# Kept block weights reread on ScalarE instead of GpSimd, and block weights made in six pieces

## The chip, the cores and the metric

The kernel runs on one NeuronCore of a Trainium2 chip. Times are device microseconds of one execution; of several runs the median is given. TensorE (PE) does the matrix products, VectorE (DVE), ScalarE (ACT) and GpSimd (POOL) the element work; SyncE (SP), ScalarE and GpSimd issue DMA transfers. Each engine works through its own instructions in order, and an instruction that waits holds up those behind it.

## The reference

For 2048 tokens of width 512 the output is a gated sum of a linear attention and a feed-forward network (FFN):

```python
g = sigmoid((x * gate_w).sum(-1))
q, k, v = split(x @ wqkv)               # 32 heads of 16
pq, pk = q @ w_phi, k @ w_phi           # per head
phi = concat(softmax(p), softmax(-p))   # for q and for k
kv, z = phi_k^T v, sum of phi_k
a = (phi_q kv) / (phi_q z + 1e-6) @ wo
b = relu(x @ w1 + b1)**2 @ w2 + b2      # 1792 hidden
out = g * a + (1 - g) * b
```

## The kernel before, in words

**Arithmetic.** Every fp32 matrix is split in a high part `h` (rounded by ScalarE, line 63) and a low part `l = x - h` (VectorE, line 66). A product is three matmuls: hh, hl, lh. `w_phi` is folded into the key weights ahead of time (`fold`), so that x times one 512 x 1024 matrix gives the 512 key features and the 512 values.

**Two sweeps.** The four blocks of 512 tokens pass through half of the hidden units in the first sweep, through the other half in the second. A work item is one block and one chunk of 128 hidden units: 12 matmuls "up" into the PSUM tile `u` (`w1`), `r = relu(u)`, its square and the split `hh`, `hl` on ScalarE and VectorE, and two items later 12 matmuls "down" into `d` (`w2`). Work is hung into this stream with `at(slot, ...)`: a slot is a half step, two to an item. In the first sweep the stream carries the keys and values, their feature map, and the sum `kv`; in the second the queries and the attention. Between the sweeps `kv` is copied, transposed (`kvt`), and the folded query weights are made (`foldq`).

**Seven products in place of eight.** Keys and values are computed by pairs of token chunks, `n` and `m = n + 2`, eight pairs. A pair is a 2 x 2 block product (2 token chunks, 2 halves of the width, 2 halves of the columns), done with seven block products in the Strassen-Winograd way. The left operands are blocks of x and sums of them (`sums`: x rows loaded to `in`, four adds on GpSimd, split into `sh` and `sl`). The right operands are blocks `a, b, c, d` of the weights and sums of them, made once in `joint`: 1 is a, 2 is c, 3 is d, 5 is b-a, 7 is d-b, 6 and 4 are longer sums. Each comes in two halves `j` of 128 rows, each with a high and a low part (512 KB together). The order of the products in a pair is 1, 2, 6, 5, 7, 3, 4 at half steps 0, 1, 1.5, 2.5, 3, 3.5 and 4.5 of the pair, and a pair takes 5. They accumulate in two PSUM tiles, X (1, 6, 5, 3) and Y (2, 7, 4). After each product X or Y is read out: 1, 6, 5 and 3 by ScalarE alone, 2, 7 and 4 by VectorE, which adds an earlier readout.

**Held and kept.** SBUF holds four of the seven weights (`HELD`). The three `KEPT` ones are stored to DRAM (`wkeep`) and reread for each pair into three slots, `sloto_332`, `sloto_333` and `slotez` (tiles that the second sweep uses otherwise). Six halves rotate through three slots, so a slot that served half number s next serves half s + 3. `again` (line 496) is called after each half product, and its DMA is issued by GpSimd, which also does the adds of `sums`, the scaling of the features (line 280) and two subtractions per half in `joint`.

**Who sets the order.** The code's order gives priorities; a scheduler in the recording layer then orders each engine's instructions by what it expects to be ready, so an instruction can stand ahead of one that was written before it. `high_priority` moves instructions forward. DMA completions share eight semaphores for SP and ScalarE together, so an issue can also wait for an earlier transfer with the same semaphore. After `joint` the `u` tile has a single PSUM bank: the next up products wait until `r` (line 370) has read the last.

Of the kernel before, what the change touches and what calls it, by code (L numbers as in the profile page):

```python
# [16 lines left out]
P = 128  # L17
# [12 lines left out]
HELD = 1, 2, 5, 3  # L30
KEPT = 6, 7, 4
# [3 lines left out]
def tile_gated_mix(ctx: ExitStack, tc: tile.TileContext, xT, xn, wqT, wkT, wphi, wv, wo, w1, b1, w2, b2, gw, out):  # L35
# [133 lines left out]
    def joint(loaded, j):  # L169
        wph, *t = loaded  # L170
        two = lambda a: a.rearrange("p (h c) -> p h c", h=2)
        raw = st["raw"]

        def whole(k):
            ps = bank(f"fold{k}")
            for g in range(NK):
                nc.tensor.matmul(ps[:, g * P:(g + 1) * P], t[g][:, k * P:(k + 1) * P], wph[:, g * P:(g + 1) * P],
                                 start=True, stop=True)
            nc.scalar.activation(two(raw[k])[:, :, :256], two(ps), AF.Copy)

        def operand(i, src, slot=None):
            if i in HELD:
                w, k = "ab"[i > 2], 2 * (HELD.index(i) % 2) + j
                hi, lo = (wpool.tile([P, 512], F32R, tag=f"w{w}{hl}{k}", name=f"w{i}{j}", bufs=1) for hl in "hl")
            else:
                hi, lo = both(st["slots"][slot])
            split(src, hi, lo, nc.scalar, nc.vector)
            st["W"][i, j] = hi, lo
            if i in KEPT:
                nc.gpsimd.dma_start(wkeep[KEPT.index(i), j], st["slots"][slot].bitcast(F32))  # L190

        def sub(eng, o, a, b):
            eng.tensor_tensor(o, a, b, ALU.subtract)

        whole(j)
        whole(2 + j)
        a, b = both(raw[j])
        c, d = both(raw[2 + j])
        operand(1, a)
        operand(2, c)  # L200
        sub(nc.vector, a, b, a)
        sub(nc.gpsimd, b, d, b)
        operand(5, a)
        sub(nc.vector, a, d, a)
        operand(3, d)
        sub(nc.gpsimd, c, c, a)
        operand(7, b, 1)
        operand(4, c, 2)
        operand(6, a, j)
# [190 lines left out]
    def do_joint(j):  # L400
        if j == 0:
            joint_start(st["wT"])
        with tc.issue_after(st["up"].ins):
            joint(st["wT"], j)
        if j == 1:
            banks[:] = [ps_a]
            again(KEPT[1], 0, 2)

# [69 lines left out]
    def sums(p):  # L478
        b, c = divmod(p, 2)
        rows = xT[b].rearrange("p k (h c r) -> p k h c r", h=2, c=2)[:, :, :, c, :]  # L480
        a, d = (stage.tile([P, 2, 2, P], F32, tag="in", name="in") for _ in range(2))
# [287 lines left out]
```

## Time and profile before

| | |
|---|---|
| runs | 543.34, 543.04, 542.16 us; median 543.04 |
| profiled execution | 541.55 us, its span 539.8 us |
| TensorE | 514.8 us busy (95%), 3427 matmuls |
| VectorE | 404.1 us (75%) |
| ScalarE | 257.3 us (48%) |
| GpSimd | 142.6 us (26%) |
| rereads of kept weights | 46 of 512 KB, all issued by GpSimd |

In the profile's rows "PE", "DVE", "ACT", "POOL" are the engines, L511 is a line of the kernel, `p<-sloto,sh` is output and inputs with buffer numbers left out. `sloto` stands for two of the slots, `slotez` for the third. "wkeep" is the copy in DRAM. A wait is put down to what came last.

### The profile page before, as it was taken

Reading aid. Unit: us, or ns where it says so; the run is one execution under the profiler, and the core shown is the slowest. Engines: PE = TensorE matmul, PEld = TensorE weight load, DVE = VectorE, ACT = ScalarE, POOL = GpSimd, SP = SyncE. Lnnn points to the kernel's source line nnn. Section 1 sums busy time; section 2 is a strip of 40 time slices with the busy share of each in tenths; the row PEclk is TensorE's granted clock in tenths of the full one; section 3 lists DMA queues with packets and bytes.
Section 4 is the critical chain, followed back from the end, with each engine's and each line's share of the span. In section 5 each row is a group of like instructions: output and inputs, shape, how many; then the busy total and the mean of one; then the engine's idle time right before and its main releaser. Section 6 shows DMA issues by size and latency. Waiting matters only on the chain.

```text
span 539.8 us, 9228 instructions
## 1 busy us (share of the span) xinstructions
PE 514.8 (95%) x3427; PEld 411.8 (76%) x3427; DVE 404.1 (75%) x682; ACT 257.3 (48%) x454; POOL 142.6 (26%) x149
## 2 busy tenths in 40 slices
PE   8978879997999979999899999999999999999997
PEld 4866658886888858878687887878787878888775
DVE  4599498776478636686798779899789887788723
ACT  3985544554345434354555473555444534343540
POOL 2045444155514271422030322121212020111100
PEclk9998979999999989999999999999999999999999
DMA  7968665655266545495438313124311321023112
GB/s 258 301 221 277 210 215 211 197 180 195 80 223 225 178 145 207 137 306 199 139 75 255 102 45 94 46 96 137 84 41 49 100 75 45 15 83 94 31 30 78
DMA packets 47284, 76.64 MB, mean 142 GB/s; under 512 B 6792, under 2 KB 22664, under 8 KB 47240
## 3 DMA queue, kind: packets, MB, share of 16 engines
q1 hardware_dynamic: 39288, 48.39, 28.9%
q0 software_dynamic: 7520, 27.27, 14.7%
q8 instruction: 27, 0.44, 0.3%
q10 hardware_dynamic: 432, 0.39, 0.2%
q14 instruction: 17, 0.14, 0.1%
HBM read 58.20 MB, written 11.54 MB: 129 GB/s over the span
## 4 chain that ended last, share of the span: by engine, by line
PE 60%; DMA 14%; DVE 12%; ACT 5%; issue 4%; POOL 3%; SPq 0%; DVEq 0%; POOLq 0%
PE u L71 6%; PE d L71 6%; PE d L72 6%; PE d L73 6%; PE u L72 6%; PE u L73 6%; DMA in<-in_xT 4%; DMA in<-in_w 3%; DMA slotez<-wkeep 3%; PE q L71 3%; PE att L71 3%; PE att L72 3%; PE att L73 3%; PE q L73 3%; PE q L72 3%
## 5 line engine op out<-in xcount | busy, mean ns | idle before, releaser
L71 PE MATMUL u<-xh,w1h 128*128 128x512 f32 x220 | 88.0, 400 | 5.5 <-ACT r L370 2.8
L299 POOL TENSOR_TENSOR ez<-e,z 128x512 f32<-128x512 f32 x32 | 41.8, 1326 | 183.3 <-ACT e L271 183.3
L71 PE MATMUL d<-w2h,hh 128*128 128x512 f32 x224 | 88.6, 395 | 0.0
L72 PE MATMUL d<-w2l,hh 128*128 128x512 f32 x224 | 88.2, 394 | 0.0
L73 PE MATMUL d<-w2h,hl 128*128 128x512 f32 x224 | 88.1, 393 | 0.0
L72 PE MATMUL u<-xl,w1h 128*128 128x512 f32 x220 | 86.3, 392 | 0.0
L73 PE MATMUL u<-xh,w1l 128*128 128x512 f32 x220 | 85.9, 391 | 0.2 <-DVE w1l L66 0.2
L370 ACT ACTIVATE r<-u,b1c 128x512 f32<-128x512 f32 x56 | 38.3, 684 | 96.4 <-PE u L73 92.9
L66 DVE TENSOR_TENSOR hl<-r,hh 128x512 fp32r<-128x512 f32 x56 | 45.6, 814 | 23.6 <-ACT hh L63 23.6
L71 PEld LDWEIGHTS u<-xh,w1h 128*128 128x128 f32 x220 | 41.5, 189 | 18.6 <-ACT r L370 3.8
L71 PEld LDWEIGHTS d<-w2h,hh 128*128 128x128 f32 x224 | 42.8, 191 | 9.3 <-issue 0.4
L73 PEld LDWEIGHTS d<-w2h,hl 128*128 128x128 f32 x224 | 42.6, 190 | 9.1
L72 PEld LDWEIGHTS d<-w2l,hh 128*128 128x128 f32 x224 | 42.6, 190 | 8.9
L73 PEld LDWEIGHTS u<-xh,w1l 128*128 128x128 f32 x220 | 41.6, 189 | 9.5 <-DVE w1l L66 0.6
L323 ACT ACTIVATE phiT<-tb 32x256 f32<-32x256 f32 x64 | 26.5, 414 | 46.1 <-DVE tb L317 45.5
L72 PEld LDWEIGHTS u<-xl,w1h 128*128 128x128 f32 x220 | 41.6, 189 | 8.0
L274 DVE TENSOR_REDUCE sm<-e 128x64 f32<-128x1024 f32 x27 | 32.8, 1214 | 17.7 <-ACT e L271 17.7
L271 ACT ACTIVATE e<-e 128x1024 f32<-128x1024 f32 x27 | 28.6, 1057 | 21.0 <-DVE e L269 19.1
L63 ACT ACTIVATE hh<-r 128x512 fp32r<-128x512 f32 x56 | 35.2, 628 | 1.2
L371 ACT ACTIVATE r<-r 128x512 f32<-128x512 f32 x56 | 35.1, 626 | 1.1
L280 POOL TENSOR_TENSOR e<-e,r 128x1024 f32<-128x1024 f32 x11 | 22.8, 2071 | 28.5 <-DVE r L276 28.4
L301 DVE TENSOR_REDUCE dz<-ez 128x64 f32<-128x1024 f32 x16 | 19.3, 1204 | 10.9 <-POOL ez L299 10.9
(170 smaller groups left out, 1020.6 us busy)
## 6 DMA issues: line engine op xcount, KB each, us to landing
sloto<-wkeep POOLq DMA_DIRECT2D x30, 512.0 KB, 4.8
in<-in_xT SPq DMA_DIRECT2D x48, 256.0 KB, 4.2
slotez<-wkeep POOLq DMA_DIRECT2D x16, 512.0 KB, 4.5
in<-in_w SPq DMA_DIRECT2D x24, 256.0 KB, 3.3
phiT<-tb SPq DMA_DIRECT2D x192, 32.0 KB, 1.9
row<-in_xn SPq DMA_DIRECT2D x16, 256.0 KB, 3.9
part<-row SPq DMA_DIRECT2D x16, 256.0 KB, 3.8
row<-part SPq DMA_DIRECT2D x16, 256.0 KB, 3.2
```

The source lines that it names most:

```text
L63: i = nc.scalar.activation(hi, src, AF.Copy)
L66: elo.tensor_tensor(lo, src, hi.bitcast(F32), ALU.subtract)
L71: nc.tensor.matmul(o, ah[:, sa], bh[:, sb], start=first, stop=False)
L72: nc.tensor.matmul(o, ah[:, sa], bl[:, sb], start=False, stop=False)
L73: return nc.tensor.matmul(o, al[:, sa], bh[:, sb], start=False, stop=last)
L271: nc.scalar.activation(ef, ef, AF.Exp)
L274: nc.vector.tensor_reduce(sm, e3, AX.X, ALU.add)
L280: eng.tensor_tensor(e3, e3, w.unsqueeze(2).to_broadcast([P, 2 * H, DH]), ALU.mult)
L299: nc.gpsimd.tensor_tensor(ez[:, hs, :], e3[:, hs, :], zbc[half], ALU.mult)
L323: nc.scalar.activation(dst, src, AF.Copy)
L370: nc.scalar.activation(r, ps, AF.Relu, bias=b1c[:, fc:fc + 1])
L371: nc.scalar.activation(r, r, AF.Square)
```

## The change

Three things change. The kept weights are now those of products 1, 6 and 3, which ScalarE reads out; `again` is called once per product, after the readout, rereads two halves, and its DMAs are issued by ScalarE. `joint` is cut in three pieces for each half j, and the six pieces are called at half steps 3, 4, 5, 6, 7 and 8 where two calls stood at 3 and 4. The pairs start at half step 9.5 + 5p where it was 8.5 + 5p; the load of x for `sums` has a call of its own at the half step at which it was, and the adds come 1.5 half steps later.

```diff
-HELD = 1, 2, 5, 3
-KEPT = 6, 7, 4
+HELD = 2, 4, 5, 7
+KEPT = 1, 6, 3
...
+    def joint(j, piece):
+        if piece == 0:
+            whole(j)
+            whole(2 + j)
         a, b = both(raw[j])
         c, d = both(raw[2 + j])
-        operand(1, a)
-        operand(2, c)
-        sub(nc.vector, a, b, a)
-        sub(nc.gpsimd, b, d, b)
-        operand(5, a)
-        sub(nc.vector, a, d, a)
-        operand(3, d)
-        sub(nc.gpsimd, c, c, a)
-        operand(7, b, 1)
-        operand(4, c, 2)
-        operand(6, a, j)
+        if piece == 0:
+            operand(3, j, d, j)
+            operand(1, j, a, j)
+            sub(nc.vector, a, b, a)
+            sub(nc.gpsimd, b, d, b)
+        elif piece == 1:
+            operand(5, j, a)
+            operand(2, j, c)
+            sub(nc.vector, a, d, a)
+        else:
+            operand(7, j, b)
+            sub(nc.gpsimd, c, c, a)
+            operand(4, j, c)
+            operand(6, j, a, 2)
...
-    def again(i, j, slot):
-        t = st["slots"][slot]
-        nc.gpsimd.dma_start(t.bitcast(F32), wkeep[KEPT.index(i), j])
-        st["W"][i, j] = both(t)
+    def again(p, i):
+        for j in range(2):
+            step = 2 * KEPT.index(i) + j
+            nxt, t = step + 3, st["slots"][step % 3]
+            if nxt < 6 or p < NB * NC // 2 - 1:
+                k, jj = KEPT[nxt % 6 // 2], nxt % 2
+                nc.scalar.dma_start(t.bitcast(F32), wkeep[KEPT.index(k), jj])
+                st["W"][k, jj] = both(t)
...
-            if i in KEPT:
-                step = 2 * KEPT.index(i) + j
-                nxt = step + 3
-                if nxt < 6 or p < NB * NC // 2 - 1:
-                    again(KEPT[nxt % 6 // 2], nxt % 2, step % 3)
...
+            if i in KEPT:
+                again(p, i)
...
-        at(s - 1 - (p > 0), sums, p)
+        at(s - 2 - (p > 0), sums_load, p)
+        at(s - 1.5 if p else s - 0.5, sums, p)
...
-    at(3, do_joint, 0)
-    at(4, do_joint, 1)
+    for slot, j, piece in ((3, 0, 0), (4, 1, 0), (5, 0, 1), (6, 1, 1), (7, 1, 2), (8, 0, 2)):
+        at(slot, do_joint, j, piece)
...
-        pair_steps(p, 8.5 + 5 * p)
+        pair_steps(p, 9.5 + 5 * p)
```

In the slots, half 0 of weight 3, then half 0 of weight 1 pass through `sloto_332`, their halves 1 through `sloto_333`; both halves of weight 6, first 1, then 0, through `slotez`. Each is stored to DRAM by GpSimd before the next overwrites it.

GpSimd, in the first sweep at the sums of two later pairs, before:

```order
L280 TENSOR_TENSOR e<-e,r 128x1024
L486 TENSOR_TENSOR in<-in 128x2x128 x2
L487 TENSOR_TENSOR in<-in 128x2x128 x2
L488 TENSOR_TENSOR in<-in 128x2x128 x2
L489 TENSOR_TENSOR in<-in 128x2x128 x2
L498 DMA slotez<-wkeep 128x1024
L498 DMA sloto_332<-wkeep 128x1024
L498 DMA sloto_333<-wkeep 128x1024
```

and at such a place in the changed kernel:

```order
L280 TENSOR_TENSOR e<-e,r 128x1024
L488 TENSOR_TENSOR in<-in 128x2x128
L489 TENSOR_TENSOR in<-in 128x2x128
L280 TENSOR_TENSOR tmp<-tmp,r 128x1024
L490 TENSOR_TENSOR in<-in 128x2x128
L491 TENSOR_TENSOR in<-in 128x2x128
```

The rereads have left GpSimd's queue. They stand on ScalarE, here at products 1 and 6 of pair 1 (line 548 reads a product out):

```order
L548 ACTIVATE tmp<-p_831 128x512
L504 DMA sloto_332<-wkeep 128x1024
L504 DMA sloto_333<-wkeep 128x1024
L271 ACTIVATE e<-e 128x1024
L370 ACTIVATE r<-u,b1c 128x512
L371 ACTIVATE r<-r 128x512
L63 ACTIVATE hh<-r 128x512
L504 DMA slotez<-wkeep 128x1024
L548 ACTIVATE tmp<-p_831 128x512
L504 DMA sloto_332<-wkeep 128x1024
```

The first two are issued after the readout of product 1, the third ahead of that of product 6; it waits for TensorE alone.

ScalarE where the weights are made, in the changed kernel, from the split of the second half of weight 1 on (`sh` are the sums of pair 0; `w_517`, split from `tmp` here, is half 1 of weight 4, `slotez` half 1 of weight 6):

```order
L63 ACTIVATE sloto_333<-tmp 128x512
L63 ACTIVATE w_542<-raw_335 128x512
L63 ACTIVATE sh<-in 128x512 x2
L370 ACTIVATE r<-u,b1c 128x512
L63 ACTIVATE w_477<-tmp 128x512
L371 ACTIVATE r<-r 128x512
L63 ACTIVATE w_512<-tmp 128x512
L63 ACTIVATE hh<-r 128x512
L63 ACTIVATE w_547<-raw_337 128x512
L63 ACTIVATE slotez<-tmp 128x512
L63 ACTIVATE w_517<-tmp 128x512
L370 ACTIVATE r<-u,b1c 128x512
```

Before, 18 splits and folds stood in one run ahead of a single `r`; now two `r` lie within this stretch, the first behind `sh`, the second behind `w_517`. A little further on the first reread of weight 3 and the split of `slotez` from `raw_335` (half 0 of weight 6) stand between the readout of product 1 and the reread of weight 6:

```order
L548 ACTIVATE tmp<-p_595 128x512
L504 DMA sloto_333<-wkeep 128x1024
L63 ACTIVATE slotez<-raw_335 128x512
L504 DMA sloto_332<-wkeep 128x1024
L238 ACTIVATE ge<-lg 128x1 x2
```

All four are new at this place.

60 lines of the change are left out of this document (28 added, 32 removed).

## The prediction, on record before the changed kernel ran

> **What bounds the kernel now.** I read the page's table of engines first.
>
> ```profile
> span 539.8 us, 9228 instructions
> ...
> PE 514.8 (95%) x3427; PEld 411.8 (76%) x3427; DVE 404.1 (75%) x682; ACT 257.3 (48%) x454; POOL 142.6 (26%) x149
> ```
>
> TensorE is busy 95%, so only its 25 us of idle time, and time in which it runs slowly, can be won. The waits of TensorE name the idle time.
>
> ```profile
> PE p L511 <- DMA slotez<-wkeep: 6.1, 3, 3.1
> PE p L511 <- DMA sloto<-wkeep: 4.0, 2, 3.7
> PE u L71 <- ACT r L370: 2.8, 1, 2.8
> PE u L71 <- ACT w1h L63: 2.6, 2, 1.9
> PE foldq L146 <- ACT r L370: 1.6, 1, 1.6
> ...
> PE p L513 <- DVE sl L66: 1.0, 1, 1.0
> PE p L511 <- DVE vext L537: 0.6, 1, 0.6
> PE kvt L597 <- DVE row L586: 0.5, 1, 0.5
> ```
>
> The columns are total, times, longest. Ten microseconds are waits for rereads of kept weights; 6.5 (2.8 + 1.9 + 1.0 + 0.6, and 0.2 below) fall where block weights are made and pair 0 runs; 2.2 (1.63 + 0.53) in the turn to the second sweep. The rest lies in the kernel's first 10 us. TensorE's timeline shows where, and what follows a wait (start, duration, in brackets the idle time before).
>
> ```profile
> 35.01 0.39 PE L72 MATMUL d<-w2l,hh 128*128 128x512 f32 x1
> 38.18 0.51 PE L71 MATMUL u<-xh,w1h 128*128 128x512 f32 x1 [2.78 <-ACT r L370]
> ...
> 45.18 0.50 PE L71 MATMUL u<-xh,w1h 128*128 128x512 f32 x1 [1.90 <-ACT w1h L63]
> ...
> 46.35 0.50 PE L73 MATMUL u<-xh,w1l 128*128 128x512 f32 x1 [0.21 <-DVE w1l L66]
> ...
> 50.34 0.40 PE L71 MATMUL u<-xh,w1h 128*128 128x512 f32 x1
> ...
> 75.05 0.80 PE L511 MATMUL p<-slotez,xh 128*128 128x512 f32 x1 [2.44 <-DMA slotez<-wkeep]
> ...
> 81.06 0.40 PE L513 MATMUL p<-w,xl 128*128 128x512 f32 x1
> ...
> 130.48 0.50 PE L511 MATMUL p<-slotez,xh 128*128 128x512 f32 x1 [3.13 <-DMA slotez<-wkeep]
> 130.81 0.39 PE L512 MATMUL p<-slotez,xh 128*128 128x512 f32 x1
> 131.04 0.39 PE L513 MATMUL p<-slotez,xl 128*128 128x512 f32 x1
> ...
> 193.25 0.57 PE L511 MATMUL p<-sloto,sh 128*128 128x512 f32 x1 [3.66 <-DMA sloto<-wkeep]
> ...
> 197.00 0.40 PE L71 MATMUL d<-w2h,hh 128*128 128x512 f32 x1
> ...
> 235.28 0.50 PE L511 MATMUL p<-slotez,xh 128*128 128x512 f32 x1 [0.56 <-DMA slotez<-wkeep]
> ```
>
> A matmul follows the one before by 0.23 us (130.81 to 131.04). After three of the waits it follows at about 0.4: from 46.35 to 50.34 lie 10 steps (4.0 us instead of 2.3), from 75.05 to 81.06 lie 14 (6.0 instead of 3.2), from 193.25 to 197.00 lie 9 (3.75 instead of 2.0). These slow stretches cost 1.7 + 2.8 + 1.7 = 6.3 us. With 18.8 us of waits between 27 and 300 us (10.1 + 6.5 + 2.2), that is **25.1 us to be won**, and a microsecond of waiting costs on average 1.33.
>
> The rereads are late because of GpSimd, as its timeline shows ("DMA_DIRECT2D" is the issue).
>
> ```profile
> 70.04 1.07 POOL L489 TENSOR_TENSOR in<-in 128x256 f32<-128x256 f32 x1
> 71.05 0.55 POOL L498 DMA_DIRECT2D slotez<-wkeep  x1
> ...
> 126.15 0.57 POOL L498 DMA_DIRECT2D slotez<-wkeep  x1
> ...
> 185.62 0.74 POOL L486 TENSOR_TENSOR in<-in 128x256 f32<-128x256 f32 x1 [11.05 <-DMA in<-in_xT]
> ...
> 189.25 0.55 POOL L498 DMA_DIRECT2D sloto<-wkeep  x1
> ...
> 228.21 0.53 POOL L498 DMA_DIRECT2D slotez<-wkeep  x1 [4.52 <-PE p L513]
> ```
>
> Before 71.05, 126.15 and 189.25 the issue stands behind the adds of a later pair's x, the last of which waited 11 us for x. Those three issues precede the waits that end at 75.05, 130.48 and 193.25. Only the fourth, at 228.21, was issued at once; its transfer took 7.0 us and cost 0.56.
>
> **The change, part by part.** *Rereads, pairs 1 to 7.* Some 45 issues leave GpSimd's queue, and with it the adds. ScalarE issues them; in its order the urgent one of two stands in front of the product's readout (waiting for TensorE alone) or right behind it. What the transfer needs:
>
> ```profile
> DMA to landing us min/median/max: 3.6/4.7/7.7
> ...
> L449 ACTq DMA_DIRECT2D row<-in_w x2: 408/434/459, 0.7 to 1.2; - x2
> ```
>
> The first row is line 498's own, the second the only ScalarE issues that the trace has from the start of a row. From the end of a kept product to the second half that its slot serves next, the new order of TensorE has 27 to 30 matmuls, 6.1 to 6.8 us at 0.227. No 512 KB load on ScalarE's queue is in this trace. Its landing is bounded by the row's 3.6 and 7.7; I take 4.7, the same bytes. Issue (0.43) and landing make 5.1, so most fit, and the waits of pairs 1 to 7 (3.13 + 3.66 + 0.56) go. For 14 such loads I keep 1.5 us, some 0.1 each (bounds 0, and 14 x 1.9 = 27 at 7.7). ScalarE pays 45 x 0.43 = 19 us, hidden in the time in which it waits for TensorE:
>
> ```profile
> ACT r L370 <- PE u L73: 92.9, 28, 8.1
> ```
>
> Without that cover r, and with it the single PSUM bank of the up products, would come 0.4 us later per issue.
>
> The Trainium skill ("DMA: Bandwidth & Descriptors", section "Anatomy of one DMA — SWDGE (gpsimd) path") fits a transfer as 2.0 us and its bytes at 436 GB/s, an estimate of 3.2 us for 512 KB; the row above says 4.7. By the page's figure the 1.5 us would be nothing and the time 2 us lower; I go by the row.
>
> *Weights in six pieces.* The work is the same (14 splits, 4 folds, 8 subtractions), later and spread. What it runs into:
>
> ```profile
> 26.24 0.59 ACT L179 ACTIVATE raw<-fold 128x512 f32<-128x512 f32 x1
> ...
> 37.46 0.67 ACT L370 ACTIVATE r<-u,b1c 128x512 f32<-128x512 f32 x1
> ...
> 41.07 1.67 POOL L193 TENSOR_TENSOR tmp<-tmp 128x512 f32<-128x512 f32 x1 [1.05 <-DVE tmp L193]
> ...
> L488 POOL TENSOR_TENSOR in<-in x8: 729/907/1229, 51.9 to 192.4; 128x256 f32<-128x256 f32 x8
> ...
> in<-in_xT SPq DMA_DIRECT2D x48, 256.0 KB, 4.2
> ...
> wkeep<-slotez POOLq DMA_DIRECT2D x2, 512.0 KB, 4.0
> ```
>
> (a) 18 activations stood from 26.24 to the r at 37.46; 13 do now, at some 0.55 us, with waits for two weight loads: r at about 34.1, done 34.8. TensorE comes there 5 matmuls sooner, at 34.1. The 2.78 becomes 0.7. The 1.9 and 0.2 for w1h go, since its staging buffer now comes free when xl is split, ahead of the weights' splits.
>
> (b) The next r now stands behind both sh splits of pair 0, and these behind GpSimd's four adds. x for them is issued near 33.5 when w2's split frees the buffer, lands 4.2 later, four adds take 4 x 1.1 (upper half of their row, since VectorE is busy too): the second sh is done near 43, r near 43.8. TensorE finishes up at 37.6 and 12 down matmuls at 40.3, a wait of 3.5. With the better adds (4 x 0.75) it is 1.7; I take 2.6 (bounds 0 and 4.5).
>
> (c) The r after it stands behind w4's second split, this behind a GpSimd subtraction (1.67), this behind the adds of pair 1: one more 4 x 1.1 and a third subtraction after 43, so r near 52; TensorE, which has 18 matmuls for cover, waits 1.5 (bounds 0 and 4).
>
> (d) Product 6 of pair 0 needs its second half from DRAM. It is stored by GpSimd right after (c)'s subtraction (4.0 to landing); ScalarE, in order, waits for that store to overwrite the slot with the first half, and only then issues the reread, behind the reread of product 3: 52 + 0.6 + 4 for the store, 0.6 for the split, 4.7 and a little more for the load, near 62. TensorE, which goes on at 53 after (c), is there 21 matmuls later, about 58. I take 3.8 (bounds 0 and 6). This takes the place of the old 0.35 (the rest of "sloto") and 2.44, and the 1.0 for sl and 0.6 for vext go with their later products.
>
> *Pairs half a step later.* This gives (b) to (d) the little cover that they have. At the far end it takes cover away: kv of the last pair now ends 13 matmuls, 3 us, before the transposition that needs it, where it had 20.
>
> ```profile
> 283.94 1.71 DVE L586 COPY row<-kvps 17x256 f32<-17x256 f32 x4
> ```
>
> The copies between them take 1.71 behind whatever VectorE has queued. For that and the folds of q I keep 2.0 of the old 2.2 (bounds 0.5 and 5).
>
> **Sum.** New waits 0.7 + 2.6 + 1.5 + 3.8 + 1.5 + 2.0 = 12.1, with the slow stretches x 1.33 = 16.1. The profiled execution took 541.55 (539.8 and 1.75 around it): 541.55 - 25.1 + 16.1 = 532.6. The median of the runs, 543.04, lies 1.5 above it: **534 us**.
>
> The slow stretches need a word. In the rows, 1.9 and 0.2 brought one, 2.78 and 3.13 none. The Trainium skill ("TensorE: Matmul & The Clock Gate", section "Why this matters for your kernels") has the clock drop only after gaps of more than about 3 us. The trace agrees for 3.66 and not for 1.9 or 3.13. By the page's rule only (d) would bring one, 1.7 us in place of 4, and the time would be 532; I go by the average of the rows.
>
> **The rivals.**
>
> *The new wait stays short* (0.14). GpSimd's adds run faster than my estimate, so that (b) to (d) vanish: 0.7 + 1.5 + 2.0 = 4.2, x 1.33 = 5.6, 541.55 - 25.1 + 5.6 + 1.5 = 523.5. For it: the scheduler put those instructions there because it expects them in time. Against it: VectorE, the third column of times below, was busy 13.19 of 13.5 us there, and its work is the same.
>
> ```profile
> 27.00:40.50 13.50, 10.72 (x56) 8.82 (x55) 13.19 (x18) 11.73 (x22) 6.22 (x6) 1.00 0.63 220
> ```
>
> *All of the making's waits stay* (0.15). (a) to (d) at their upper bounds, 0.7 + 4.5 + 4 + 6, with 1.5 and 2.0: 18.7 x 1.33 = 24.9, time 543, no change. For it: the chain through GpSimd, a store and a load is new and serial. Against it: four bounds at once.
>
> *The reread lands late from ScalarE's queue* (0.14), the slower case. Place: the second halves of products 6 and 1, 14 times. Cover is 6.4 us on average less 0.43, so beyond a landing of 5.9 each further microsecond costs 14 x 1.33 = 18.6 us. It eats my gain of 9 at a mean landing of about 6.5 (1.5 us are in the sum already); at 6.8 the time is 14 x 0.9 x 1.33 - 2 = 15 us above mine, 549. For it: 7.0 at 228.21, when x was loading too, and two loads now start together. Against it: the median of 46 loads.
>
> The skill's page on DMA (section "Issuing engines are not separate DMA queues") has all issuers share the same engines, so the landing should not change with the issuer; no run here shows it yet.
>
> That the change does not do what it says is shut out by the order of GpSimd and ScalarE.
>
> **How the numbers follow.** Forecast 0.57, with its own range 527 to 540 (one of (b) to (d) at a bound either way). From the rivals, 523.5 weighs 0.14, 543 0.15 and 549 0.14. The range of 8 in 10 is 523.5 to 543.5. A measurement of this kernel tells a change from none at about 0.2%, 1.1 us. Faster: 0.57 + 0.14 + a third of 0.15 = 0.76. Same: 0.07. Slower: 0.14 and the rest of 0.15, 0.17.
>
> **What would show it.** Steps that are right: no wait of TensorE for wkeep over 1 us after pair 0; no reread issue on GpSimd; landings of ScalarE's rereads near 4.7; one wait for wkeep in pair 0's product 6 near 4 us; waits of u for r near 2.6 and 1.5 behind sh and w4. Wrong: many waits for wkeep of about a microsecond (third rival), or r waiting for ScalarE's transfers elsewhere in the sweep, which I have costed at nothing.

## The result, and the profile after

The changed kernel takes 546.89 us (median of 20 runs, 541.99 to 549.48), the kernel before 542.06 us beside it (20 runs, 538.28 to 545.38). The ratio is 1.0079, with a 95% interval of 1.0055 to 1.0104: **slower by 0.8%**, a small change, but the interval leaves out 1. 534 us was forecast. The profiled execution took 546.88 us.

The page's table of engines, of the changed kernel:

```profile
span 545.1 us, 9200 instructions
...
PE 516.5 (95%) x3427; PEld 414.3 (76%) x3427; DVE 410.6 (75%) x682; ACT 257.4 (47%) x454; POOL 117.5 (22%) x103
```

GpSimd lost 25 us of work, as intended, and TensorE gained nothing: it is idle 28.6 us (25.0 before) and busy 1.7 us longer for the same number of matmuls. In what follows `r` names two things: the relu of line 370, for which the up products wait, and the reciprocal of line 276, by which GpSimd scales the features. The waits of TensorE (total, times, longest):

```profile
PE u L71 <- ACT r L370: 8.8, 4, 3.7
PE kvps L289 <- POOL e L280: 7.5, 2, 5.4
PE kvt L601 <- DVE row L590: 3.4, 1, 3.4
PE kvps L289 <- issue: 1.2, 1, 1.2
...
PE p L517 <- DMA sloto<-wkeep: 0.9, 2, 0.6
```

The 10.1 us of waits for rereads are 0.9. Two rows are new as waits: 7.5 us in which the kv products (`kvps`, line 289) wait for the scaling of the features by `r` (line 280, GpSimd), and 3.4 us for the transposes at the turn. A third is a gap: 1.2 us ahead of the last two of pair 0's 128 kv matmuls, for which the profile names no releaser ("issue"); the scaling for them had ended at 96.4, and a gap of 0.9 to 1.1 us stays there in e5, e12 and e18 below, which change the order or drop loads. TensorE's timeline has the places, and the slow stretches behind them (start, duration, idle time before):

```profile
37.73 0.50 PE L71 MATMUL u<-xh,w1h 128*128 128x512 f32 x1 [3.32 <-ACT r L370]
...
46.26 0.50 PE L71 MATMUL u<-xh,w1h 128*128 128x512 f32 x1 [1.17 <-ACT r L370]
...
57.10 0.79 PE L71 MATMUL u<-xh,w1h 128*128 128x512 f32 x1 [3.75 <-ACT r L370]
...
62.39 0.63 PE L71 MATMUL u<-xh,w1h 128*128 128x512 f32 x1
...
65.48 0.50 PE L517 MATMUL p<-sloto,sh 128*128 128x512 f32 x1 [0.56 <-DMA sloto<-wkeep]
...
98.35 0.23 PE L289 MATMUL kvps<-e,vext 128*17 128x32 f32 x2 [1.20 <-issue]
...
128.71 1.06 PE L289 MATMUL kvps<-e,vext 128*17 128x32 f32 x64 [5.44 <-POOL e L280]
129.69 0.80 PE L517 MATMUL p<-w,sh 128*128 128x512 f32 x1
...
134.13 0.63 PE L72 MATMUL u<-xl,w1h 128*128 128x512 f32 x1
...
207.26 0.73 PE L289 MATMUL kvps<-e,vext 128*17 128x32 f32 x64 [2.01 <-POOL e L280]
...
291.29 0.41 PE L601 MATMUL kvt<-ident,row 128*128 128x128 f32 x2 [3.42 <-DVE row L590]
```

From 57.10 to 62.39 lie 12 steps (5.3 us instead of 2.7), from 129.69 to 134.13 lie 10 (4.4 instead of 2.3); two more stretches, behind the waits that end at 37.73 and 291.29, cost some 1.5 each. In all the slow stretches cost about 8 us, 6.3 before. Idle time up by 3.6 and slow time up by some 2 make the 5.3 us by which the span grew.

How far TensorE has come by 65 us shows in the busy time between 27 and 65 us; the first figure behind the stretch's length is TensorE's, with its matmuls. The kernel before:

```profile
27.00:65.00 38.00, 31.75 (x136) 24.55 (x135) 31.76 (x63) 25.56 (x50) 19.89 (x21) 0.96 0.71 236
```

and the changed kernel:

```profile
27.00:65.00 38.00, 29.69 (x115) 22.91 (x113) 34.71 (x56) 23.79 (x46) 22.56 (x22) 0.87 0.64 213
```

It is 21 matmuls behind, 4.8 us at 0.227. So nearly the whole loss against the kernel before arises while the weights are made. From there on the rereads' waits go, and waits for kv and for the turn take their place.

How the longest of them comes about can be followed backwards. GpSimd's timeline:

```profile
120.44 0.74 POOL L488 TENSOR_TENSOR in<-in 128x256 f32<-128x256 f32 x1 [1.97 <-DMA in<-in_xT]
...
125.24 0.72 POOL L488 TENSOR_TENSOR in<-in 128x256 f32<-128x256 f32 x1 [0.85 <-DMA in<-in_xT]
126.05 0.72 POOL L489 TENSOR_TENSOR in<-in 128x256 f32<-128x256 f32 x1
126.72 1.93 POOL L280 TENSOR_TENSOR e<-e,r 128x1024 f32<-128x1024 f32 x1
```

Six adds, four for pair 3 and two for pair 4, stand ahead of the scaling of pair 1, and wait for their x. VectorE's timeline shows that `r` for this scaling was done at 122.2, and why it was no sooner:

```profile
106.22 0.69 DVE L236 SCALAR_TENSOR_TENSOR row<-row,gwb 128x512 f32<-128x512 f32 x1 [4.42 <-DMA row<-in_xn]
...
116.90 2.11 DVE L66 TENSOR_TENSOR sl<-in,sh 128x512 fp32r<-128x512 f32 x1
...
121.65 0.54 DVE L276 RECIPROCAL r<-sm 128x64 f32<-128x64 f32 x1
```

VectorE stood 4.4 us at a row of the gate (`in_xn`, line 236), with the pair's readouts and splits queued behind. SyncE issued these rows late, behind loads of x, and the x of pairs 3 and 4 later still, since their staging buffers are free only after VectorE's splits `sl` (for which SyncE waits there):

```profile
99.63 1.74 SPq L81 DMA_DIRECT2D in<-in_xT  x2
101.42 5.86 SPq L231 DMA_DIRECT2D row<-in_xn  x3
113.01 6.43 SPq L482 DMA_DIRECT2D in<-in_xT  x4
```

### The profile page after: what moved, and what is told of

Same layout as the page of the kernel before. It is cut to its first block, busy times and chain, and to the rows that moved or that the text cites. A ratio compares the mean times of both kernels' runs of the same rounds, so it can differ in the third digit from the quotient of the medians.

```text
span 545.1 us, 9200 instructions
## 1 busy us (share of the span) xinstructions
PE 516.5 (95%) x3427; PEld 414.3 (76%) x3427; DVE 410.6 (75%) x682; ACT 257.4 (47%) x454; POOL 117.5 (22%) x103
## 4 chain that ended last, share of the span: by engine, by line
PE 57%; DVE 18%; DMA 12%; ACT 4%; POOL 4%; issue 4%; SPq 1%; ACTq 0%; DVEq 0%; POOLq 0%
PE u L71 6%; PE d L71 6%; PE d L73 6%; PE d L72 6%; PE u L72 6%; PE u L73 5%; DMA in<-in_xT 3%; DMA in<-in_w 3%; DVE sl L66 3%; PE att L73 3%; PE att L71 3%; PE q L72 3%; PE q L73 3%; PE q L71 3%; PE att L72 3%
## 5 line engine op out<-in xcount | busy, mean ns | idle before, releaser
L71 PE MATMUL u<-xh,w1h 128*128 128x512 f32 x220 | 89.4, 406 | 9.0 <-ACT r L370 8.8
L72 PE MATMUL u<-xl,w1h 128*128 128x512 f32 x220 | 87.7, 399 | 0.0
L73 PE MATMUL u<-xh,w1l 128*128 128x512 f32 x220 | 87.4, 398 | 0.0
L66 DVE TENSOR_TENSOR hl<-r,hh 128x512 fp32r<-128x512 f32 x56 | 42.4, 757 | 23.5 <-ACT hh L63 23.5
L280 POOL TENSOR_TENSOR e<-e,r 128x1024 f32<-128x1024 f32 x11 | 24.0, 2179 | 87.7 <-DVE r L276 71.2
L271 ACT ACTIVATE e<-e 128x1024 f32<-128x1024 f32 x27 | 28.6, 1059 | 24.5 <-DVE e L269 22.7
L723 DVE SCALAR_TENSOR_TENSOR row<-d,rest,row 128x512 f32<-128x512 f32 (+1 forms) x33 | 22.5, 726 | 7.8 <-PE d L73 7.8
```

The source lines that it names most:

```text
L66: elo.tensor_tensor(lo, src, hi.bitcast(F32), ALU.subtract)
L71: nc.tensor.matmul(o, ah[:, sa], bh[:, sb], start=first, stop=False)
L72: nc.tensor.matmul(o, ah[:, sa], bl[:, sb], start=False, stop=False)
L73: return nc.tensor.matmul(o, al[:, sa], bh[:, sb], start=False, stop=last)
L271: nc.scalar.activation(ef, ef, AF.Exp)
L280: eng.tensor_tensor(e3, e3, w.unsqueeze(2).to_broadcast([P, 2 * H, DH]), ALU.mult)
```

## The experiments

The theories that the expectations name: **A**, the adds on GpSimd, which run up to two pairs ahead, stand ahead of the scaling for kv. **B**, the loss comes from the pairs' half step or the weight pieces. **C**, ScalarE's DMA issues hold up the exponentials. **D**, VectorE is late in any case, since its list waits for rows of the gate. Every ratio below is to the kernel before on the same chip. The runs are of several chips, on which the kernel before took 541.2 to 544.3 us, so runs are compared by their ratios; a difference of two medians can be off by up to 3 us.

| run | kernel | median us | ratio, 95% interval |
|---|---|---|---|
| | changed kernel | 546.9 | 1.0079 (1.0055 to 1.0104) |
| e1 | changed, sums back behind their loads | 543.0 | 0.9975 (0.9934 to 1.0017) |
| e2 | changed, pairs half a step earlier | 536.7 | 0.9872 (0.9816 to 0.9929) |
| e3 | changed, rereads by GpSimd | 550.1 | 1.0102 (1.0046 to 1.0158) |
| e4 | before, rereads by ScalarE | 534.0 | 0.9830 (0.9770 to 0.9890) |
| e5 | changed, adds in order | 541.9 | 0.9998 (0.9967 to 1.0030) |
| e6 | e4, pairs late | 535.8 | 0.9889 (0.9827 to 0.9952) |
| e7 | e2, pieces bunched | 533.0 | 0.9826 (0.9771 to 0.9882) |
| **e8** | **e4, adds in order** | **524.1** | **0.9668 (0.9620 to 0.9716)** |
| e9 | before, adds in order | 540.3 | 0.9973 (0.9947 to 0.9999) |
| e10 | changed, pairs early, bunched, adds in order | 534.0 | 0.9834 (0.9784 to 0.9884) |
| e11 | changed, pairs early, adds in order | 532.7 | 0.9822 (0.9778 to 0.9866) |
| e12 | changed, bunched, adds in order | 541.0 | 0.9975 (0.9948 to 1.0003) |
| e13 | e8, six pieces | 531.1 | 0.9782 (0.9732 to 0.9833) |
| e14 | e8, pairs late | 536.1 | 0.9852 (0.9805 to 0.9898) |
| e15 | e8, both | 537.2 | 0.9889 (0.9849 to 0.9929) |
| e16 | e14 without rows of the gate | 527.7 | 0.9747 (0.9706 to 0.9789) |
| e17 | e8 without rows of the gate | 524.7 | 0.9694 (0.9655 to 0.9732) |
| e18 | changed, without rows of the gate | 535.0 | 0.9883 (0.9841 to 0.9925) |

### One part undone, one part alone (e1 to e4)

**e1**, against the changed kernel:

```diff
-        at(s - 1.5 if p else s - 0.5, sums, p)
+        at(s - 2 - (p > 0), sums, p)
```

> The changed kernel with the adds and splits of every pair's sums put back right behind their loads, as the kernel before had them; rereads, weight pieces and pairs stay as changed. Theory A (GpSimd works its list in order, and the later adds, which wait for their loads, stand ahead of the scaling by r that the kv products wait for): the kv products' wait for GpSimd, 7.5 us in two places, falls under 2 us, the slow matmuls behind the 5.4 us wait go with it, and the time falls by 7 to 10 us, to 537 to 540. Theory B (the loss comes from the pairs' half step or from the weight pieces): the time stays within 1.5 us of the changed kernel's 546.9. Theory C (ScalarE's six DMA issues a pair hold up the exponentials): the same as B, and the wait of the kv products stays.

543.0 us, 1.0% below the changed kernel's ratio, and a partial answer: the kv products wait 4.0 us (3.2 + 0.8) where they waited 7.5, and 3.5 us of waits for rereads came up (0.9). This edit takes away about half of the wait, and the time lies between the ranges; neither A nor B holds alone.

**e2**, against the changed kernel:

```diff
-        pair_steps(p, 9.5 + 5 * p)
+        pair_steps(p, 8.5 + 5 * p)
```

> The changed kernel with every pair one half step earlier, as before; the sums keep their place relative to the pair. Theory A: the adds stand in the same place relative to the scaling, so the kv products still wait 4 to 8 us; only the 3.4 us wait of the transposes behind the last kv products falls to 0.5, as in the kernel before, and the time is 542 to 545. Theory B (the half step itself is the loss): 538 to 541, kv waits gone. Either way the waits for the weights' making can only grow, since pair 0 starts one half step sooner: 8.8 us of waits for r becomes 9 to 12.

536.7 us, under both ranges (2.1% below the changed kernel by the ratios). The kv products' waits are 2.0 us and the transposes' 0.5; the waits in the making grew as expected, to 5.0 for `r` and 7.1 for weight 6, and yet the kernel is faster. It does not refute A: in this kernel's trace the next adds begin at 123.79, behind the scaling of pair 1 at 121.66.

**e3**, against the changed kernel:

```diff
-                nc.scalar.dma_start(t.bitcast(F32), wkeep[KEPT.index(k), jj])
+                nc.gpsimd.dma_start(t.bitcast(F32), wkeep[KEPT.index(k), jj])
```

> The changed kernel with the rereads issued by GpSimd again, two at the end of each product, in the changed order of the kept weights. If ScalarE as the issuer is what took away the 10.1 us of waits for rereads (my prediction's term), 6 to 10 us of such waits come back, and the time is 553 to 559. If the order of the products and their pairing is enough, the waits for rereads stay under 2 us and the time within 1.5 us of 546.9. Theory C (ScalarE's issues hold up the exponentials) alone says faster: 540 to 544, with the kv wait under 2 us.

550.1 us; its waits of TensorE:

```profile
PE p L517 <- DMA sloto<-wkeep: 11.9, 4, 5.8
PE u L71 <- ACT r L370: 7.5, 3, 3.8
```

The waits for rereads are back at 11.9 us, so ScalarE as issuer is what removed them. But the time rose by 0.2% only, under the range and less than the runs can tell: the kv products now wait for nothing. **A wait for a reread covers the scaling behind which kv would wait: take the first away and the second appears.** C is not decided here: the kv wait goes, as C says too, but the time is no lower, since the rereads' waits are back. It falls with e5 and e8, in which ScalarE issues the rereads and the kv products wait 1.2 and 1.1 us for the scaling.

**e4**, against the kernel before:

```diff
-        nc.gpsimd.dma_start(t.bitcast(F32), wkeep[KEPT.index(i), j])
+        nc.scalar.dma_start(t.bitcast(F32), wkeep[KEPT.index(i), j])
```

> The kernel before with nothing changed but the engine that issues the rereads: ScalarE instead of GpSimd. My prediction's term (10.1 us of waits for rereads, each us worth 1.33 with its slow matmuls) stands alone here: 528 to 531 if the waits go and nothing takes their place. The rival (the time that is won is waited elsewhere, for r and for the weights' making, in the steps that follow): waits for rereads under 2 us, other waits up by 5 us or more, and a time of 537 to 542.

534.0 us, between the two ranges. Of the waits of TensorE:

```profile
PE kvps L289 <- POOL e L280: 6.1, 3, 3.9
...
PE p L511 <- DMA slotez<-wkeep: 1.2, 1, 1.2
```

The rereads' 10.1 us are 1.4, and 6.1 us of waits of the kv products stand where there were none. One word of the diff wins 1.7%; the rest of the change loses 2.5%.

### The order of the adds (e5, e8, e9)

**e5**, against the changed kernel (`scaled` and `phi` record the instruction; the loads of x stay where they were):

```diff
-        add(d1, a1, d1, ALU.add)
-        add(a1, a0, a1, ALU.subtract)
-        add(a0, d1, a0, ALU.subtract)
-        add(d0, d0, a0, ALU.subtract)
+        with tc.issue_after((st["scaled", p - 2] if p > 1 else st["up"]).ins):
+            add(d1, a1, d1, ALU.add)
+            add(a1, a0, a1, ALU.subtract)
+            add(a0, d1, a0, ALU.subtract)
+            add(d0, d0, a0, ALU.subtract)
...
                 v["phi", t] = scaled(e3, r, nc.gpsimd)
+                st["scaled", p] = st["scaled"]
```

> The changed kernel with one order added on GpSimd: the four adds of pair p's sums come behind the scaling of pair p - 2, and so never two pairs ahead of their use. Same operations, same half steps. Theory A (adds for pairs 3 and 4, waiting for their loads, stand ahead of the scaling of pair 1): the kv products' wait for GpSimd, 7.5 us, falls to 1.5 us or less, the slow matmuls behind it go too, and the time is 536 to 540. Theory D (VectorE is late with r in any case, since its list waits 4.4 us for a row of the gate): r itself is late, the kv products still wait 3 us or more, as they did for 4.0 us with the sums put back, and the time is 542 to 546. A new wait for the split sums (sl) of 1 to 3 us would show that the adds now come too late.

541.9 us, ratio 0.9998 against 1.0079. The waits of TensorE:

```profile
PE u L71 <- ACT r L370: 7.9, 3, 3.5
PE p L518 <- DMA sloto<-wkeep: 4.4, 2, 3.5
PE kvt L603 <- DVE row L592: 3.5, 1, 3.5
PE p L518 <- DVE vext L539: 2.1, 1, 2.1
PE kvps L289 <- POOL e L280: 1.2, 1, 1.2
```

The kv products' wait for the scaling fell to 1.2 us as A says. The time fell less than A says: 4.4 us of waits for rereads came up, 3.5 of them for weight 6 in pair 0, and 2.1 us for a readout by VectorE. That last wait would fit D; this run does not show its cause.

**e8** is e4 with the edit of e5, the load of x split off but at its old half step.

> The kernel before with ScalarE issuing the rereads and the adds of pair p put behind the scaling of pair p - 2, nothing else. Theory A: of the 6.1 us that the kv products wait with ScalarE's rereads alone, 4 us or more go, and the time falls from 534.0 to 527 to 531. Theory D: the kv products wait as before and the time stays at 533 to 536.

524.1 us, better than the expectation: 3.3% under the kernel before, 4.1% under the changed one, and the fastest kernel of this study. Its waits of TensorE, and the stretch from 27 to 65 us:

```profile
PE u L71 <- ACT r L370: 2.8, 1, 2.8
PE u L71 <- ACT w1h L63: 2.2, 2, 2.0
...
PE kvps L289 <- POOL e L280: 1.1, 1, 1.1
PE p L515 <- DMA slotez<-wkeep: 1.1, 1, 1.1
```

```profile
27.00:65.00 38.00, 33.06 (x144) 26.25 (x142) 32.24 (x58) 24.90 (x48) 17.18 (x18) 0.96 0.79 258
```

All waits of kv but one are gone, hardly a new one came up (0.6 us for a readout), and one slow stretch is left in the sweep (1.4 us). TensorE has done 144 matmuls by 65 us, 29 more than in the changed kernel.

**e9** is the edit of e5 on the kernel before, with GpSimd still issuing the rereads.

> The kernel before, its rereads still issued by GpSimd, with the adds of pair p put behind the scaling of pair p - 2 and nothing else. It divides the gain of the fastest kernel so far (524.1 us: this order and ScalarE's rereads together) between the two. If the rereads were late only because adds for later pairs, which wait for their loads, stood ahead of their issues, the order alone takes away most of the 10.1 us of waits for rereads and the time is 526 to 531. If GpSimd is too slow an issuer in any case (its scalings, which wait for r, stand ahead of the issues as well), waits for rereads of 5 us or more stay, and the time is 533 to 541.

540.3 us, 0.3% under the kernel before: the waits for rereads are as the first theory has them, 2.7 us, the time is in the range of the second. The kv products wait 2.5, `foldq` 2.5 for `r`, and readouts by ScalarE cost 3.4. So ScalarE's issue alone is worth 1.7%, the order of the adds alone 0.3%, both together 3.3%: with one alone, other waits take up what it wins.

### The half step and the six pieces, with the adds in order (e6, e7, e10 to e15)

**e6** is e4 with `pair_steps(p, 9.5 + 5 * p)`.

> The kernel before with two edits: ScalarE issues the rereads, and every pair comes one half step later. Against ScalarE's rereads alone (534.0 us) it shows the half step by itself, without the six pieces and without the later adds. If the half step is what costs (theory B): 541 to 546, with 3 us of wait for the transposes behind the last kv products and more waits of the kv products than 6.1 us. If it costs only together with the later adds (theory A): 533 to 537, the transposes' 3 us and their slow matmuls aside.

535.8 us, 0.6% above e4 by the ratios, within their intervals. The transposes wait 2.9 us, as expected, but the kv products' wait of 6.1 us is 0.5. Here GpSimd's adds before that scaling run from 101.96 on, where e4 has them from 109.45, and the scaling comes in time. That this hides a part of the half step's price fits e14, where nothing hides it; no run shows it by itself.

**e7** is e2 with the pieces called at two half steps, in the same order:

```diff
-    for slot, j, piece in ((3, 0, 0), (4, 1, 0), (5, 0, 1), (6, 1, 1), (7, 1, 2), (8, 0, 2)):
+    for slot, j, piece in ((3, 0, 0), (3, 0, 1), (4, 1, 0), (4, 1, 1), (4, 1, 2), (4, 0, 2)):
```

> The changed kernel with the pairs at their old half step and the six pieces of the weights' making bunched at half steps 3 and 4 instead of 3 to 8, in the same order of pieces. Against the pairs put back alone (536.7 us) it shows the spreading by itself. If the spreading is a loss (the last piece comes so late that pair 0 waits 7.1 us for the weights of product 6): that wait falls under 2 us, the waits for r stay near 5, and the time is 528 to 532. If the spreading helps, as I predicted (each relu waits less): the waits for r rise by 3 us or more, and the time is 535 to 540.

533.0 us against 536.7, with overlapping intervals: the wait for weight 6 fell from 7.1 to 3.7 us and the waits for `r` stayed (4.9 against 5.0), but kv waits 3.6 in place of 2.0. The run misses both theories, and the times give no clear verdict.

**e10, e11, e12** are the changed kernel with the adds in order (e5), and the pairs, the pieces or both put back.

> The changed kernel with three things put back or in order: pairs at their old half step, six pieces bunched at half steps 3 and 4, adds behind the scaling of pair p - 2. What is left of the change is ScalarE as issuer, the other choice of kept weights, and the order in which the weights are made. Against 524.1 us (the kernel before with ScalarE's rereads and the same order of adds) it shows what the choice of weights is worth. If nothing: 523 to 526. If the new order of making is a loss (weight 6 is made last, and pair 0 needs it third: 3.7 us of wait with the pieces bunched): 527 to 532, with that wait still there.

> The changed kernel with the pairs at their old half step and the adds behind the scaling of pair p - 2; the six pieces stay spread over half steps 3 to 8. Two comparisons: against the same order of adds with the pairs late (541.9 us) it is the half step alone, against the run with the pieces bunched as well it is the spreading alone. If the half step costs by itself (transposes 3 us, and more): 531 to 536. If it gives cover to the making, as I predicted: pair 0 waits 5 us or more for weight 6, and the time is 537 to 542. Spreading: a loss if this is 3 us or more above the bunched one.

> The changed kernel with the pieces bunched at half steps 3 and 4 and the adds behind the scaling of pair p - 2; the pairs stay one half step late. Against 541.9 us (pieces spread) it is the spreading alone with pairs late. If spreading costs (each late piece makes relu or product 6 of pair 0 wait): the waits for r (7.9 us) and for the reread of weight 6 in pair 0 (3.5 us) fall by 5 us or more together, and the time is 531 to 536. If it is harmless: 539 to 543.

In e11 pair 0 waits 5.2 us for weight 6, as was expected of an early pair, and the time is the lower one all the same. With the adds in order the four make a square (medians, us):

| new choice of weights | pairs early | pairs late |
|---|---|---|
| pieces bunched | 534.0 (e10) | 541.0 (e12) |
| pieces spread | 532.7 (e11) | 541.9 (e5) |

The half step costs 7 and 9 us (1.4% and 1.8% by the ratios), the spreading nothing that the runs can tell. And e10 is above e8 (524.1), and above its own ranges: **1.7% by the ratios, 9 us**. What differs is the choice of the kept weights with the order in which they are made; with it go the rereads, two at a time behind the readout, and for the sums x loaded one half step earlier and added half a one later. Its stretch from 27 to 65 us:

```profile
27.00:65.00 38.00, 28.02 (x113) 21.90 (x113) 31.62 (x54) 22.12 (x42) 18.62 (x18) 0.87 0.72 235
```

113 matmuls against 144: 31 of them, 7.0 of the 9 us. TensorE waits 6.6 us in three places for `r` and 3.4 for weight 6, with 3.3 us of slow matmuls after them; weight 6 is made last there, and pair 0 needs it third.

**e13** is e8 with its weights made in six pieces in their old order (1 and 2; 5 and 3; 7, 4 and 6); **e14** is e8 with pairs late; **e15** has both:

```diff
-    at(3, do_joint, 0)
-    at(4, do_joint, 1)
+    for slot, j, piece in ((3, 0, 0), (4, 1, 0), (5, 0, 1), (6, 1, 1), (7, 0, 2), (8, 1, 2)):
+        at(slot, do_joint, j, piece)
```

> The fastest kernel so far (the kernel before, ScalarE's rereads, adds behind the scaling of pair p - 2: 524.1 us) with its weights made in six pieces at half steps 3 to 8, in its own order and with its own choice of kept weights. It shows the spreading by itself. If the changed kernel lost its 7 us before 65 us by the spreading: TensorE has done 115 to 120 matmuls between 27 and 65 us instead of 144, and the time is 530 to 535. If it lost them by the new choice and order of weights (weight 6 last and needed third, its second half through DRAM): 135 to 145 matmuls, 522 to 527.

> The fastest kernel so far (524.1 us) with every pair one half step later, nothing else. The half step alone: it costs the wait for the transposes (2.9 us with 1.3 of slow matmuls after it, as in the earlier run with ScalarE's rereads) and nothing more if kv and the rereads keep their cover: 526 to 530. If the half step brings pairs and the gate's rows together on VectorE (8 to 9 us, as it did with the new choice of weights): 531 to 535.

> The fastest kernel so far (524.1 us) with both: six pieces spread over half steps 3 to 8 and every pair one half step later, the old choice and order of weights. If the two edits add up from the two runs beside this one, spreading and half step do not depend on each other, and what is left to 541.9 us (the changed kernel with the same order of adds) is the price of the new choice and order of weights. If the half step gives cover to the spread making, this is faster than the spreading alone.

| old choice of weights | pairs early | pairs late |
|---|---|---|
| two calls | 524.1 (e8) | 536.1 (e14) |
| pieces spread | 531.1 (e13) | 537.2 (e15) |

Here the spreading alone costs 7 us (1.1% by the ratios, 6 us): 116 matmuls between 27 and 65 us.

```profile
27.00:65.00 38.00, 29.59 (x116) 22.90 (x116) 34.95 (x61) 22.34 (x44) 17.33 (x18) 0.83 0.69 229
```

TensorE waits 4.5 us there for one `r`, at 53.72. In ScalarE's list splits stand ahead of it, and wait in turn: those of pair 0's sums 4.1 us for the adds, and one of a piece 2.4 for a store of a kept weight that must be finished before its slot is written again. In e8 such waits (3.9 and 1.4 us) stand ahead of an `r` as well, at 55.57, but TensorE has down products and products of pair 0 to do until 57.06 and waits for none of it. The half step alone costs 12 us (1.8% by the ratios, 10 us), more than either theory had. Both together cost 13 us (2.2%, 12), less than the sum, but the runs do not tell this clearly from a sum.

### The rows of the gate (e16 to e18)

Where the half step costs, e14's timelines show. VectorE:

```profile
227.26 0.69 DVE L236 SCALAR_TENSOR_TENSOR row<-row,gwb 128x512 f32<-128x512 f32 x1 [7.96 <-DMA row<-in_xn]
```

and TensorE after it:

```profile
232.96 0.47 PE L515 MATMUL p<-w,xh 128*128 128x512 f32 x1 [1.91 <-DVE vext L541]
```

VectorE stands 8 us at one row (4.7 in e8), and 5.7 us later a product waits for the readout `vext`, which stood in VectorE's list behind that row. (A later wait, 1.8 us at 243.37, is for a readout by ScalarE, which stood behind a split that waited 2.3 us for its load of x.) In all VectorE waits 13.2 us for rows of the gate (4.7 in e8, 14.0 in e6, 8.1 in the changed kernel, 9.9 in the kernel before). The test takes the loads of these rows away for token chunks 4 to 15, and their gate is computed from `gwb` alone, so that the three kernels leave out a part of the function:

```diff
-        nc.sync.dma_start(st["xn", n], xn[n])
+        if n < NC:
+            nc.sync.dma_start(st["xn", n], xn[n])
...
-        nc.vector.scalar_tensor_tensor(t, t, 1.0, gwb, op0=ALU.mult, op1=ALU.mult, accum_out=lg)
+        nc.vector.scalar_tensor_tensor(t, t if n < NC else gwb, 1.0, gwb, op0=ALU.mult, op1=ALU.mult, accum_out=lg)
```

> The run with the half step alone (pairs late, ScalarE's rereads, adds in order, old weights: 536.1 us), without the loads of the gate's rows of token chunks 4 to 15; the gate of those chunks is computed from the gate's weights in place of the row, by the same number of instructions. VectorE then waits for no row (13.2 us there, 8.0 of them at one place). If the half step costs because VectorE's list stands at these rows while products wait to be read out: 527 to 531, at most 4 us above the same edit with the pairs early. If its cost has another source: 532 to 536.

> The fastest kernel so far (524.1 us, pairs early) with the same loads of the gate's rows left out (the gate of chunks 4 to 15 from the gate's weights). It takes out what the missing transfers are worth by themselves: VectorE waited 4.7 us for a row there, in one place, behind which TensorE lost about 1 us. 521 to 524 under either theory; the difference of the two runs against the 12 us between the same two with rows is what counts.

527.7 and 524.7 us. With pairs early the rows cost nothing; with pairs late they cost 8 us (1.1% by the ratios, 6 us), and the half step is left at 3.1 us of its 12 (2.9 of 10). The waits for readouts are those that go, in e14:

```profile
PE p L515 <- ACT tmp L551: 3.1, 2, 1.8
...
PE p L515 <- DVE vext L541: 2.5, 2, 1.9
```

and in e16:

```profile
PE p L516 <- DVE vext L542: 0.6, 1, 0.6
PE p L516 <- ACT tmp L552: 0.6, 1, 0.6
```

So most of the half step's cost hangs on the rows, as D says. The transfers go with the rows; e17 loses the same ones and gains nothing, but with pairs late no run separates the two.

> The changed kernel itself, without the loads of the gate's rows of token chunks 4 to 15 (their gate is computed from the gate's weights). VectorE waited 8.1 us for such rows, 4.4 of them from 101.8 to 106.2 us, ahead of the pair whose scaling came 5.4 us late for the kv products. If the rows carry a large part of the loss here too: the 5.4 us wait falls to 2 us or less and the time is 536 to 541. If the adds on GpSimd alone make that wait (they wait for their own loads): it stays above 3.5 us, and the time is 543 to 547.

535.0 us, 2.0% below the changed kernel by the ratios, 11 us. Of its waits of TensorE (its scaling is line 281):

```profile
PE kvps L290 <- POOL e L281: 0.4, 1, 0.4
```

The waits of kv for the scaling are gone (7.5 to 0.4), though the adds of pair 3 still stand among the scalings of pair 1. This fits that the adds do harm where their x comes late, and that x comes late where VectorE, held by a row, frees its buffers late. But the run is not a clean one, and its 11 us are no measure of the rows' wait alone: with them go 3 MB of transfers, and in GpSimd's order the scaling of pair 1 moved ahead of pair 4's adds. What the adds' order and the rows cost together in the changed kernel was not run.

## Why the prediction was wrong, step by step

**Rereads: right.** "The waits of pairs 1 to 7 go" held: no wait for wkeep over 0.4 us after pair 0, and the "1.5 us" kept for the steady state was 0.4. The rival of late landings fell with the row of line 504:

```profile
L504 ACTq DMA_DIRECT2D sloto<-wkeep x30: 326/326/598, 59.7 to 244.7; - x30
...
DMA to landing us min/median/max: 3.4/4.5/7.1
```

The median is 4.5 us (4.7 taken), an issue 0.33 (0.43 taken). That ScalarE's issues are hidden also held (C fell in e5 and e8; in e8 the up products wait 2.8 us for `r`, as before). The Trainium skill ("DMA: Bandwidth & Descriptors", section "Issuing engines are not separate DMA queues") has DMAs run on the same 16 DMA engines whichever engine started them; the trace's landings agree, 4.5 us from ScalarE's queue and 4.7 from GpSimd's.

**Making of the weights: right in sum by luck, wrong in its places, and its baseline was not worked out.** (a) to (d) were 0.7, 2.6, 1.5 and 3.8, together 8.6 us; measured were 3.32, 1.17, 3.75 and 0.56, together 8.8. Each was off by 1.4 to 3.2 us, two up and two down. In (a) `r` stood behind a split that waited 2.1 us for a load of w1, and in (c) behind splits that waited 2.2 us for a subtraction on VectorE and 2.8 for one on GpSimd, which stood behind the adds of pair 1. (d) was short since TensorE came to it late. With the slow stretches the forecast lost 11.4 us there, and 38 us less 115 matmuls at 0.227 gives 11.9. Before had 6.2 + 1.7 us in that stretch, so the step was a loss of 3.5 us by my own numbers (4.8 measured); the sum hid it behind the rereads' gain. The runs add what I did not ask: the spreading costs 6 to 7 us with the old weights (e13 against e8), and by 65 us the kernel with the new choice and order is 7 us behind (e10 against e8).

**The step that failed: what the rereads' waits covered.** In "25.1 us to be won" each wait that goes was won whole, and the sum had no term for the kv products, whose chain (readout, exponentials on ScalarE, `r` on VectorE, scaling on GpSimd) had been on time only because TensorE was late: e3, with those waits, has no wait for kv, and e4, without them, has 6.1 us. Measured: 7.5 us of waits and 2.2 of slow matmuls behind the longest, 9.7 of the 12.9 us between forecast and result. The order of GpSimd that I showed had adds ahead of line 280, and I priced the issues that leave this queue but not the scaling that stays in it. In e4 10.1 us of waits become 1.4, and the 6.1 come up at once. e5 and e8 show that the order of the adds removes most of it (7.5 to 1.2, and 6.1 to 1.1), and e18 that it also goes with the rows and their transfers.

**Turn between the sweeps: mis-sized.** 2.0 us was taken, 2.7 with slow matmuls (bounds 0.5 and 5); measured were 3.4 and 1.4 of slow matmuls. That is 2.1 us more. With the 9.7, and the 1.2 us gap that no releaser explains, this is 13.0 us, the size of the miss; the other terms were off by under 2 us each, up and down.

**Half step: wrong in sign.** It was to give cover; it costs 1.1% to 2.1%, 6 to 11 us, in five pairs of runs (the changed kernel against e2, e5 against e11, e12 against e10, e14 against e8, e15 against e13), and 0.6% only in e6 against e4, where the kv products' wait shrank by 5.6 us. Three parts were seen: the transposes' wait, which the sum had, the adds, and the rows on VectorE, which the prediction named nowhere.

**Slow stretches at 1.33 per us of waiting: right here, as an average.** 22.9 us of waits between 27 and 300 us brought about 8 us of slow matmuls, 1.35; in e8 8.2 us of waits brought 1.4, a factor of 1.17.

What stays open: whether the choice of the kept weights, the order of making, or the half steps of the sums cost the 9 us between e8 and e10, since no run has one without the others; what the 1.2 us gap in the kv products of pair 0 is; and why the spreading costs 6 to 7 us with the old order and nothing with the new one.

## What to carry to other kernels

Before a wait is counted as won, look for what finishes during it: list the next two or three things that the waiting engine will need, and when each is ready. An order that a scheduler makes from expected times lets work for later stages stand ahead of work that is due; one dependency ("not ahead of the scaling two pairs back") was worth 1.6% here on top of the moved rereads (e8 against e4), about as much as these (1.7%), but only 0.3% without them. Test a change of three parts one part at a time: the part of one word won 1.7%, and the whole lost 0.8%.

## What the runs showed of the hardware

**The clock.** The matmul step is 0.43 instead of 0.23 us in a slow stretch, which the windows of the changed kernel show at a granted clock of 0.50:

```profile
57.10:62.40 5.30, 5.30 (x13) 4.14 (x14) 5.30 (x13) 2.65 (x6) 4.06 (x5) 0.50 0.56 201
129.69:134.13 4.44, 4.44 (x19) 3.47 (x11) 0.75 (x2) 0.00 (x0) 0.46 (x1) 0.50 0.02 4
```

Stretches of 1.0 to 3.1 us of loss followed every wait of 3.4 us or more between 27 and 300 us in these runs (3.42 to 7.11). Of shorter waits some brought one and some did not: 1.87 (e6), 2.30 (e9) and 2.95 (e2) did, 3.13 (before) and 3.33 (e7) did not. The Trainium skill ("TensorE: Matmul & The Clock Gate", section "Why this matters for your kernels") sets gaps of more than about 3 us; the runs agree above 3.4 us, and below it the measurement decides.

**VectorE beside GpSimd.** A split of 128x512 takes 0.68 us on VectorE in the second sweep. Between 45 and 58 us, where GpSimd adds and subtracts most of the time, such splits take up to 1.8 us:

```profile
L66 DVE TENSOR_TENSOR hl<-r,hh x11: 626/674/692, 308.5 to 397.5; 128x512 fp32r<-128x512 f32 x11
```

```profile
L66 DVE TENSOR_TENSOR w<-tmp,w x3: 692/1205/1780, 48.3 to 56.5; 128x512 fp32r<-128x512 f32 x3
```

Both answers are of the changed kernel, the first from 300 to 400 us, the second from 45 to 58 (shortest, median and longest in ns). The one of 0.69 us, at 56.51, fell where GpSimd had no element work; beside the other two it added or subtracted. Over the whole kernel, by the two engines' timelines, 100 splits (those listed singly) that meet no GpSimd operation took 0.62 to 0.69 us, and every longer one met one (2.11 us for the `sl` at 116.90, beside a scaling). The surplus of the two here, 0.5 and 1.1 us, is near the length of half a GpSimd add or a whole one (1.06). That VectorE's work gets longer where it is moved next to GpSimd's was not a term of the prediction; it may be part of what the spreading costs, which no run shows by itself.
